# An RWKV-5 chunk kernel with a squared-ReLU FFN: two GpSimd DMA issues moved ahead of a weight cast, and two VectorE operations moved ahead of a third

## The chip, the cores and the metric

The kernel runs on one core of one Trainium2 chip. Its time is the device time of one execution in microseconds (us). The kernel before has three timed runs: 177.46, 177.65 and 178.44, median 177.65. The engines are called as in the profile: PE (TensorE matmul; PEld is its weight load), DVE (VectorE), ACT (ScalarE), POOL (GpSimd) and SP (SyncE, which here only issues DMAs).

## What is computed

The reference has two parts. The first is a linear attention with a decaying state, for 4 batches, 8 heads, 768 steps and head size 48:

```python
for t in range(S):
    kt, vt, rt = (k[:, :, t].copy(), v[:, :, t].copy(), r[:, :, t].copy())
    cur = np.einsum('bhd,bhe->bhde', u[None] * kt, vt)
    y[:, :, t] = np.einsum('bhd,bhde->bhe', rt, state + cur)
    state = w[None, :, :, None] * state + np.einsum('bhd,bhe->bhde', kt, vt)
```

Its result, as 3072 tokens of 384 values (heads side by side), goes through a feed-forward layer with `w_in` of 384 x 2048 and `w_out` of 2048 x 384:

```python
h = np.maximum(x @ w_in, 0.0)
return (h * h @ w_out).astype(np.float32)
```

## The kernel before

The sequence is cut into 24 units: unit `i` is chunk `i // 4` (128 steps) of batch `i % 4`, all heads. For each unit the kernel loads `r`, `k` and `v` (`ld`, line 320), scales them with powers of the decay (`kh`, L336, and `rh`, L339: products with the tables that `Wk` and `Wt` made on ACT), transposes them on PE (`T`, L363, copied by `Tc`), and forms the scores (`A`, L376), which are masked by `Bm` (L384). `Y` (L392 and L394) applies them and the state to `v`; `U` (L403) gives the state's update. The term with `u` is made beside that: `P0` (r times k, L342), `P1` (times `u`, L346), `du` (its sum over a head, L349), `dv` (times `v`, L354). `xs` (L411) adds both into the tokens, `X` and `xTc` transpose them.

The feed-forward part works on groups of one unit (groups 0 and 1) or two (the rest). `F1` (L445) multiplies tokens by `W1`, which is kept as 8 slices of 256 columns in bf16. `F1.g.s` fills one PSUM bank for group `g`: in groups 0 and 1 it takes the slices `2s` and `2s+1`, in the later groups the slice `s`. `re` (L453 on ACT or L455 on DVE) takes the ReLU, `sq` (L460 on ACT, L462 or L464 on DVE) squares it. `F2.i.q` (L472) multiplies by quarter `q` of `W2`, and `os` and `out` bring the unit's result out.

The weights arrive in two ways. `lW.0.s` (L324, SP) loads slice `s` of `W1` in float32 into one of four staging buffers, `wsa`, and `cW.0.s` casts it to bf16: on ACT (L260), except slice 7, which POOL casts (L262). `W.0.2` (slice 2 of `W1`) and `W.1.0` to `W.1.3` (the quarters of `W2`) are loaded and cast by DMAs that POOL issues (L333); they wait for nothing. In the profile q1 is the DMA queue on which SP issues, and q0 the one on which POOL issues.

The order of all work is written out by hand in `ORDER` (lines 20 to 107). Each word is one step, with its engine (P, D, A, G for POOL, S for SP) and the buffer slots that it takes; each engine does its steps in that order, and the framework adds the semaphore waits for data and buffers. `Z` are matmuls of the identity without a result, in the early gaps of PE. SP's early order is loads of units 0 to 3 mixed with `lW.0.6`, then `lW.0.1`, then `lW.0.0`, `.5`, `.7`, `.4`, then `wc` (two small DMAs for the last column table), `ld.k.4`, `lW.0.3`, `ld.r.4`, `ld.k.5`, `ld.r.5`. POOL's order in front of the first change is `P0.3`, `vb.2`, `P1.3`, `dv.2`, then `cW.0.7`, `W.1.0`, `W.0.2`, `W.1.1`, `WLm` (L314, which waits for ACT), `W.1.2`, `W.1.3`. On DVE the order at the second change is `shw` (the shuffle that spreads `w`, L283), `P0.1`, `kh.1`, `rh.1`, `shu` (the shuffle that spreads `u`, L286), `kh.0`. On PE the order after the first groups is `F1.1.0`, `F1.0.0`, `F1.1.3`, `F1.0.3`, `F1.0.2`, `F1.1.2`, four groups of `F1.2`, `F2.0.0` (the first that needs `W.1.0`), `F1.0.1` (the first that needs `W.0.2`, and the first with slice 3), `F1.2.3`, `F2.1.0`, `F1.1.1`, `F1.2.0`, `F2.0.1`, and so on.

`HELD` (lines 109 to 115) tells which buffers a step's slot numbers are for: of two steps that share a buffer, the one that stands first in `ORDER` names the slot.

Of the kernel before, what the change touches and what calls it, by code (L numbers as in the profile page):

```python
# [21 lines left out]
Wk:A/1 lW.0.6:S/0 kh.1:D/0 ld.v.1:S/0 rh.1:D shu:D ld.k.3:S/3 T.1:P/0 kh.0:D/1 Z.16.5:P P1.1:G Tc.1:A/0 kh.2:D/2  # L22
rh.0:D ld.v.3:S/1 WtS:A rh.2:D P0.2:G/1 A.1:P/1/2 WkS:A T.0:P/3 lW.0.1:S/1 Z.16.5:P P1.2:D ld.r.3:S/3 Tc.0:A/1
du.1:D/0 P0.0:D/2 cW.0.6:A ld.v.0:S/2 A.0:P/0/3 dv.1:G Bm.1.1:D/0 Z.6.5:P du.2:D/1 T.2:P/2 P1.0:G Bm.1.0:D/1
ld.v.2:S/3 Z.22.5:P Tc.2:A/2 Bm.0.0:D/2 Bm.0.1:D/3 lW.0.0:S/2 vb.1:A/0 lW.0.5:S/3 kh.3:D/3 Y.1:P/1 cW.0.1:A lW.0.7:S/0
A.2:P/0/2 xs.1:D/0 Z.4.5:P P0.3:G/3 vb.3:A/1 du.0:D/2 lW.0.4:S/1 X.1:P/3 Z.8.5:P rh.3:D wc:S xTc.1:A/0 Bm.2.0:D/4
vb.0:A/2 T.3:P/1 ld.k.4:S/4 dv.0:D Y.0:P/3 Z.13.5:P Tc.3:A/3 vb.2:G/3 Bm.2.1:D/5 P1.3:G xs.0:D/1 A.3:P/0/2 X.0:P/1
cW.0.0:A U.0:P/3 dv.2:G Bm.3.0:D/1 Z.6.7:P xTc.0:A/1 du.3:D/3 lW.0.3:S/2 F1.1.0:P/0 Bm.3.1:D/0 ld.r.4:S/4 F1.0.0:P/1
re.1.0:D/0 cW.0.7:G Y.2:P/0 Y.3:P/1 re.0.0:A/1 ld.k.5:S/5 xs.2:D/2 cW.0.5:A W.1.0:G dv.3:D F1.1.3:P/0 cW.0.4:A W.0.2:G
X.2:P/2 F1.0.3:P/1 re.1.3:D/2 ld.r.5:S/5 xTc.2:A/0 W.1.1:G U.2:P/0 xs.3:D/3 F1.0.2:P/0 re.0.3:A/3 sq.1.3:D2/0 WLcol:A  # L30
X.3:P/2 F1.1.2:P/1 re.0.2:D/4 xTc.3:A WLm:G U.3:P/1 F1.2.1:P/0 re.1.2:A/5 W.1.2:G sq.0.3:A0/1 F1.2.5:P/1 re.2.1:D/2
W.1.3:G sq.0.0:A0/2 U.1:P/2 S0.2:D re.2.5:A/3 F1.2.4:P/0 sq.0.2:D2/3 cW.0.3:A S0.0:D F1.2.7:P/1 re.2.4:D/1 sq.1.0:A0/4
F2.0.0:P/1 sq.2.5:D2/5 re.2.7:A/4 S0.3:D F1.0.1:P/0 F1.2.3:P/1 re.0.1:D/0 F2.1.0:P/0 S0.1:D re.2.3:A/3 F1.1.1:P/0
sq.1.2:D2/6 sq.0.1:D2/7 ld.k.7:S/6 F1.2.0:P/1 re.1.1:A/5 F2.0.1:P re.2.0:A/0 sq.1.1:D2/8 F1.2.2:P/0 sq.2.4:A0/9
sq.2.0:D1/10 F2.1.1:P kh.4:D/4 F1.2.6:P/1 ld.v.5:S/4 rh.4:D P0.4:D/4 F2.1.2:P ld.r.7:S/6 re.2.2:D/5 P1.4:G F2.0.2:P
re.2.6:D/1 sq.2.2:A0/11 F2.1.3:P ld.v.4:S/5 kh.5:G/5 sq.2.1:A0/12 sq.2.6:D1/13 F2.0.3:P os.1:A/0 du.4:D/4 ld.k.6:S/0
T.4:P/0 sq.2.3:A0/14 rh.5:D F2.2.0:P/0 os.0:A/1 P0.5:D/0 Tc.4:A/4 ld.r.6:S/0 T.5:P/3 P1.5:D F2.2.1:P kh.7:D/6 Tc.5:A/5
# [4 lines left out]
T.6:P/0 P0.7:D/2 os.2:A/2 A.7:P/1/2 S.5:D re.3.1:A/5 ld.r.8:S/1 F2.3.3:P du.6:D/2 P1.7:G Tc.6:A/0 Bm.7.1:D/0  # L42
F1.3.3:P/0 sq.3.0:A0/16 rh.9:G ld.r.10:S/3 os.3:D/3 F1.3.4:P/1 re.3.3:A/2 Bm.7.0:D/1 A.6:P/3/0 P0.9:G/3 du.7:D/1
re.3.4:A/1 XB.9:S/1 F1.3.5:P/0 Bm.6.1:D/3 sq.3.1:A0/17 dv.7:G F1.3.6:P/1 Bm.6.0:D/2 re.3.5:A/3 F2.5.0:P/0 dv.6:G
vb.6:A/7 ld.k.12:S/5 sq.3.3:A0/18 Y.7:P/2 out.3:S kh.10:D/3 re.3.6:A/4 Y.6:P/1 ld.v.8:S/3 S.4:G xs.7:D/1 F1.3.2:P/0
sq.3.5:A0/19 xs.6:D/2 F1.3.7:P/1 ld.v.11:S/1 kh.8:D/0 re.3.2:A/0 kh.15:D/4 U.6:P/0 X.6:P/3 sq.3.2:A0/20 X.7:P/2 rh.8:D
F2.4.0:P/1 ld.r.12:S/4 re.3.7:A/5 rh.10:D F2.5.1:P xTc.6:A/2 sq.3.4:D2/21 P1.9:D xTc.7:A U.7:P/1 T.8:P/3 vb.9:A/2
out.0:S P0.8:D/4 F1.4.0:P/0 ts.6:D/1 ld.k.11:S/0 Tc.8:A/2 P1.8:G ts.7:D/0 F1.4.4:P/1 ld.r.13:S/5 du.9:D/3 re.4.0:A/2
F2.5.2:P kh.12:G/5 re.4.4:A/3 F1.4.6:P/0 ld.r.11:S/0 sq.3.6:A0/23 sq.3.7:D2/22 vb.8:G/3 du.8:D/4 A.9:P/2/0
sq.4.4:A0/24 A.8:P/1/3 S.6:G re.4.6:A/0 F2.5.3:P ld.v.10:S/5 Bm.8.1:D/4 F1.4.3:P/1 dv.8:G Bm.8.0:D/5 os.5:A/3  # L50
ld.k.13:S/6 F1.4.5:P/0 Bm.9.1:D/1 re.4.3:A/1 dv.9:G Y.8:P/3 Bm.9.0:D/0 re.4.5:A/5 XB.10:S/3 F2.4.1:P P0.12:G/0
xs.8:D/3 sq.4.0:A0/25 Y.9:P/1 vb.11:A/1 kh.11:G/1 F1.4.1:P/1 xs.9:D/4 ld.v.13:S/4 X.8:P/0 F1.4.2:P/0 re.4.1:D/4
xTc.8:A/0 ld.r.15:S/6 F2.4.2:P rh.11:D sq.4.1:A0/26 P1.12:D X.9:P/2 vb.10:A/0 F1.4.7:P/1 P0.10:D/1 ld.k.20:S/2 xTc.9:A
sq.4.5:D2/27 F2.7.0:P/0 P0.11:D/2 re.4.7:A/3 ld.v.12:S/6 U.8:P/3 P1.10:D sq.4.3:A0/28 F2.4.3:P kh.13:D/6 re.4.2:A/2
F1.5.2:P/1 du.10:D/0 out.1:S os.4:A/1 rh.13:G sq.4.2:A0/29 ts.8:D/1 A.10:P/1/0 ld.k.17:S/1 F2.6.0:P/1 re.5.2:A/4
P1.11:G ld.k.14:S/5 F1.5.7:P/0 rh.12:G F1.5.1:P/1 du.11:D/1 ld.k.16:S/4 re.5.7:A/5 T.11:P/2 rh.15:D re.5.1:A/1
F1.5.0:P/0 dv.10:G Bm.10.1:D/3 Tc.11:A/4 ld.v.14:S/0 F1.5.5:P/1 vb.13:D/4 re.5.0:A/2 Bm.10.0:D/2 dv.11:G U.11:P/3
A.11:P/0/2 XB.13:S/5 sq.4.7:A0/2 F2.7.1:P S.7:D re.5.5:A/3 Bm.11.1:D/4 P0.15:G/3 Y.10:P/1 sq.5.2:A0/4 F2.6.1:P
XB.12:S/6 du.12:D/2 sq.5.5:A0/7 Bm.11.0:D/5 U.9:P/2 F1.5.6:P/0 kh.17:D/0 F2.6.2:P ld.r.14:S/2 ts.9:D/0 re.5.6:A/4
Y.11:P/0 sq.5.0:D2/8 sq.5.1:A0/6 out.2:S S.9:G xs.10:D/0 F1.5.3:P/1 sq.4.6:A0/3 ld.r.16:S/1 xs.11:D/2 F1.5.4:P/0  # L60
re.5.3:D/3 S.8:G X.10:P/2 U.10:P/1 XB.15:S/0 F2.7.2:P xTc.10:A/1 P1.15:D vb.14:A/5 F2.7.3:P ts.10:D/0 dv.12:G
ts.11:D/1 ld.r.17:S/3 X.11:P/0 F2.6.3:P os.7:A/0 kh.16:D/1 xTc.11:A kh.14:D/2 A.13:P/2/1 re.5.4:A/2 ld.k.18:S/0
A.12:P/3/0 F1.6.2:P/1 sq.5.3:A0/0 sq.5.4:D2/1 S.10:D os.6:A/2 F1.6.3:P/0 re.6.2:A/1 rh.14:D ld.v.18:S/3 F2.9.0:P/0
re.6.3:A/0 rh.16:D F1.6.6:P/1 sq.5.6:A0/10 sq.5.7:D2/12 XB.14:S/2 P0.13:D/4 F2.9.1:P Bm.13.0:D/1 P1.13:G F1.6.1:P/0
Bm.13.1:D/0 XB.16:S/1 F2.8.0:P/1 P0.14:G/1 Bm.12.1:D/3 re.6.1:A/2 F2.8.1:P Bm.12.0:D/2 sq.6.3:A0/11 P1.14:G
ld.r.18:S/0 sq.6.1:A0/14 A.15:P/2/1 F1.6.4:P/0 vb.12:A/7 out.6:S Bm.15.0:D/5 P0.17:G/2 re.6.6:A/3 ld.v.17:S/2 U.13:P/0
Y.12:P/3 du.13:D/4 re.6.4:A/5 F2.8.2:P rh.17:G xs.12:D/1 ld.v.15:S/5 F1.6.0:P/1 Bm.15.1:D/4 A.14:P/2/3 du.14:D/3
re.6.0:A/4 xX.12:S/2 U.12:P/1 dv.13:D F2.8.3:P sq.6.2:A0/9 kh.18:D/3 F1.6.5:P/0 Bm.14.0:D/3 XB.17:S/3 F1.6.7:P/1
S.11:D re.6.5:A/0 ts.13:D/0 F2.9.2:P os.8:A/2 out.7:S P0.18:D/0 sq.6.0:A0/5 Y.13:P/2 ts.12:D/1 ld.k.21:S/3
sq.6.6:A0/13 F2.9.3:P P1.18:G xs.13:D/3 sq.6.5:A0/15 ld.v.16:S/1 F2.10.0:P/1 Bm.14.1:D/2 dv.14:G X.13:P/0 du.15:D/0  # L70
F2.10.1:P ld.r.20:S/4 P0.16:G/4 re.6.7:D/2 xTc.13:A Y.14:P/1 vb.15:A/6 F1.7.5:P/0 kh.20:G/6 xs.14:D/4 ld.k.22:S/6
os.9:A/0 F1.7.6:P/1 S.12:D A.16:P/2/3 xX.14:S/0 re.7.6:A/1 P1.17:G A.17:P/0/1 F2.11.0:P/0 sq.6.7:A0/16 Bm.17.1:D/1
sq.6.4:A0/17 S.13:G F1.7.1:P/1 ld.v.20:S/6 Bm.16.1:D/0 re.7.5:A/4 F2.11.1:P ld.k.19:S/5 Bm.17.0:D/2 dv.15:G Y.15:P/1
re.7.1:D/3 ld.r.19:S/6 F1.7.0:P/0 xs.15:D/0 rh.20:G F1.7.3:P/1 re.7.0:A/0 ld.r.23:S/5 P1.16:D U.15:P/3 sq.7.1:A0/20
F2.10.2:P du.16:D/1 re.7.3:A/2 U.14:P/0 xX.15:S F1.7.2:P/0 P0.20:D/1 vb.16:A/3 dv.16:G Bm.16.0:D/3 sq.7.3:A0/18
F1.7.4:P/1 out.5:S re.7.2:A/5 rh.18:D F2.11.2:P vb.18:A/1 out.8:S sq.7.6:D2/21 re.7.4:A/3 F2.10.3:P sq.7.5:D2/19
ld.r.21:S/2 kh.19:D/5 vb.17:A/2 F1.7.7:P/0 ld.k.23:S/1 sq.7.4:A0/22 rh.19:D Y.16:P/1 kh.22:D/4 re.7.7:A/2 Y.17:P/2
XB.19:S/4 xs.16:D/2 sq.7.2:A0/23 F2.11.3:P kh.21:D/2 os.10:A/3 F1.8.2:P/1 du.17:D/2 sq.7.0:A0/26 XB.18:S/6 ts.14:D/1
F1.8.0:P/0 dv.17:G re.8.2:A/1 F2.12.0:P/1 os.11:A/2 re.8.0:D/4 vb.20:G/0 sq.8.2:A0/25 F1.8.3:P/1 xX.16:S/1 S.14:G
sq.7.7:A0/29 F2.13.0:P/0 re.8.3:A/3 P0.19:D/3 out.10:S U.17:P/1 F2.12.1:P ts.17:D/0 kh.23:G/0 ld.r.22:S/3 F1.8.7:P/0  # L80
xs.17:D/3 out.4:S du.18:D/4 F1.8.5:P/1 re.8.7:A/5 ts.15:D/1 F2.13.1:P re.8.5:A/0 S.15:D A.19:P/0/1 sq.8.7:A0/28
P1.19:D A.18:P/2/3 F1.8.1:P/0 Bm.19.1:D/5 xX.17:S rh.21:D F2.13.2:P re.8.1:A/1 P0.21:D/4 F1.8.4:P/1 ld.v.19:S/4
sq.8.3:A0/24 rh.23:D ld.v.22:S/0 F1.8.6:P/0 Bm.18.0:D/4 ld.v.21:S/5 U.18:P/1 rh.22:D F2.12.2:P re.8.6:A/2 Bm.18.1:D/0
sq.8.1:A0/27 F2.12.3:P XB.20:S/5 Bm.19.0:D/3 re.8.4:A/5 F1.9.1:P/0 S.17:D sq.8.6:A0/3 F2.13.3:P dv.18:D XB.21:S/2
# [25 lines left out]
    A=["bA{0}0", "bA{0}1"],  # L110
    ld=["{0}{1}"],
    lW=["ws{0}{1}"], kh=["rk{0}"], P0=["P{0}"], du=["dv{0}"], vb=["vb{0}"], T=["bT{0}"], Tc=["rkT{0}"], XB=["rkT{0}"],
    Bm=["Bm{0}{1}"], Y=["bY{0}"], xs=["xs{0}"], U=["bU{0}"], ts=["ts{0}"], X=["bX{0}"], re=["hr{0},{1}"], sq=["hq{0},{1}"],
    F1=["bH{0},{1}"], os=["os{0}"], Wk=["WkP"], Wt=["WtP"],
# [422 lines left out]
```

## Time and profile before

| | |
|---|---|
| median of three timed runs | 177.65 us (177.46 to 178.44) |
| span of the profiled execution | 175.6 us, about 2 us below the timed runs |
| granted clock of PE | 1.000 |
| busy: PE, DVE, ACT, POOL | 165.1, 140.6, 109.4, 69.2 us |
| DMA moved | 28.36 MB, mean 161 GB/s |
| first F1 matmul | 20.50 us |
| first F2 matmul | 30.08 us |

The span runs from the first to the last instruction that the profiler recorded; the timed run also holds what lies around it, so that differences are compared, not absolute times. In a line of the timeline stand the start and the length in us, the engine, the line of the kernel, the operation, its output and inputs, and in brackets how long the engine was idle before it and what ended that. A line of the waits tells who waited for whom: us in total, times, the longest. Matmuls overlap in the pipeline, so that the lengths of PE rows add up to a little more than the time between their starts. In the DMA view the share of a queue is the time of its packets over the time of 16 engines; reads and writes overlap, so that it can pass 100%.

### The profile page before, as it was taken

To read this page: it belongs to the slowest core of one execution; us is meant where nothing else is said; L and a number is where in the kernel's file an instruction comes from. 1 tells how busy PE (TensorE), PEld (TensorE's weight loads), DVE (VectorE), ACT (ScalarE), POOL (GpSimd) and SP (SyncE) were. 2 spreads that over 40 slices of the span, in tenths; PEclk is the share of its full clock that TensorE was granted. 3 is DMA by queue.
4 is the path that set the end of the run, shared out by engine and by line. 5 is a ranking of instruction groups with operands and counts; after the bars stand their busy time and mean duration, and the time that the engine had idled before them with its cause. 6 is when DMAs were issued, how large, how long until landed. Compare 5 with 4: busy or idle time off the path is not lost.

```text
span 175.6 us, 4601 instructions
## 1 busy us (share of the span) xinstructions
PE 165.1 (94%) x1813; PEld 127.0 (72%) x1813; DVE 140.6 (80%) x278; ACT 109.4 (62%) x203; POOL 69.2 (39%) x84
## 2 busy tenths in 40 slices
PE   4888797899999999999999999999999999999991
PEld 4767695666778778777767787777778677787760
DVE  4699877499899998999989899899988667853620
ACT  2479498249399987886668669669478132164401
POOL 4073582035358394926282960600960302000000
PEclk9999999999999999999999999999999999999999
DMA  5999999989899999999999979989971422110041
GB/s 105 218 217 236 315 231 187 192 166 220 163 210 106 246 207 134 232 159 242 170 162 214 212 142 223 155 203 191 199 157 26 157 90 62 33 45 0 4 169 55
DMA packets 102277, 28.36 MB, mean 161 GB/s; under 512 B 94824, under 2 KB 102256, under 8 KB 102256
## 3 DMA queue, kind: packets, MB, share of 16 engines
q1 hardware_dynamic: 100360, 26.10, 75.4%
q0 software_dynamic: 1744, 1.77, 6.1%
q8 instruction: 14, 0.23, 0.6%
q10 hardware_dynamic: 152, 0.20, 0.3%
q14 instruction: 7, 0.06, 0.1%
HBM read 20.46 MB, written 4.72 MB: 143 GB/s over the span
## 4 chain that ended last, share of the span: by engine, by line
PE 80%; DMA 10%; SPq 4%; POOL 1%; issue 1%; ACT 0%; POOLq 0%
PE bank L472 36%; PE bank L445 33%; DMA wsa<-in_moe_w_in_dram 6%; DMA W<-in_moe_w_in_dram 5%; SPq L320 4%; PE bank L376 3%; PE bank L394 2%; PE bank L392 2%; PE bank L403 2%; PE bank L363 2%; PE bank L429 1%; POOL W L262 0%; SPq L324 0%; POOL W L333 0%; ACT os L260 0%
## 5 line engine op out<-in xcount | busy, mean ns | idle before, releaser
L445 PE MATMUL bank<-xT,W 128*128 128x256 bf16 (+1 forms) x624 | 74.4, 264 | 1.6 <-ACT W L260 0.9
L472 PE MATMUL bank<-W,hq 128*128 128x384 bf16 x384 | 73.6, 326 | 1.0 <-DMA W<-in_moe_w_out_dram 1.0
L453 ACT ACTIVATE hr<-bank 128x512 bf16<-128x512 f32 x71 | 42.0, 597 | 38.9 <-PE bank L445 36.3
L445 PEld LDWEIGHTS <-W 128*128 128x128 bf16 x624 | 55.3, 98 | 12.3 <-ACT W L260 1.2
L472 PEld LDWEIGHTS <-hq 128*128 128x128 bf16 x384 | 35.6, 98 | 19.0 <-issue 1.2
L460 ACT ACTIVATE hq<-hr 128x512 bf16<-128x512 bf16 x57 | 34.7, 629 | 2.5 <-DVE hr L455 2.4
L384 DVE TENSOR_TENSOR Bm<-bank,maskJT 128x512 bf16<-128x512 f32 x48 | 31.4, 683 | 3.0 <-PE bank L376 3.0
L346 POOL TENSOR_TENSOR P<-P,ub 128x384 f32<-128x384 f32 x14 | 15.2, 1086 | 35.5 <-DVE P L342 29.8
L455 DVE TENSOR_SCALAR hr<-bank 128x512 bf16<-128x512 f32 x25 | 17.1, 689 | 11.9 <-PE bank L445 8.3
L354 POOL TENSOR_TENSOR dv<-ldv,du 128x384 f32<-128x384 f32 x19 | 16.6, 886 | 23.7 <-DVE du L349 21.6
L464 DVE TENSOR_TENSOR hq<-hr 128x512 bf16<-128x512 bf16 x35 | 15.0, 457 | 1.7 <-ACT hr L453 1.7
L411 DVE TENSOR_TENSOR xs<-bank,dv 128x384 bf16<-128x384 f32 x24 | 13.2, 553 | 2.8 <-PE bank L394 2.2
L260 ACT COPY os<-bank 128x384 f32<-128x384 f32 x18 | 8.6, 477 | 8.1 <-PE bank L472 8.1
L481 PE MATMUL bank<-identity 128*128 128x128 bf16 x139 | 11.0, 242 | 2.3 <-POOL identity masks.py:199 2.3
L349 DVE TENSOR_REDUCE du<-P 128x8 f32<-128x384 f32 x24 | 12.9, 544 | 0.2 <-POOL P L346 0.2
L342 POOL TENSOR_TENSOR P<-ldr,ldk 128x384 f32<-128x384 f32 x11 | 11.3, 1024 | 2.4 <-DMA ldr<-in_r_dram 2.4
L260 ACT COPY rkT<-bank 128x1024 bf16<-128x1024 bf16 x10 | 10.1, 1015 | 2.8 <-PE bank L363 2.7
L481 PEld LDWEIGHTS <-identity 128*128 128x128 bf16 x139 | 9.7, 111 | 2.5 <-POOL identity masks.py:199 2.3
L424 POOL TENSOR_TENSOR S0W<-ts,WLm 128x384 bf16<-128x384 f32 x7 | 7.4, 1060 | 10.0 <-PE bank L472 6.7
L394 PE MATMUL bank<-vb,Bm 128*128 128x48 bf16 x192 | 10.8, 183 | 0.4 <-ACT vb L260 0.3
L394 PEld LDWEIGHTS <-Bm 128*128 128x128 bf16 x192 | 9.5, 96 | 1.4 <-issue 0.6
L260 ACT CAST vb<-ldv 128x384 bf16<-128x384 f32 x19 | 9.6, 512 | 0.0
(61 smaller groups left out, 163.8 us busy)
## 6 DMA issues: line engine op xcount, KB each, us to landing
ldr<-in_r_dram SPq DMA_DIRECT2D x24, 192.0 KB, 4.0
ldk<-in_k_dram SPq DMA_DIRECT2D x24, 192.0 KB, 4.1
ldv<-in_v_dram SPq DMA_DIRECT2D x24, 192.0 KB, 3.8
out_dram<-os SPq DMA_DIRECT2D x23, 192.0 KB, 2.1
wsa<-in_moe_w_in_dram SPq DMA_DIRECT2D x7, 384.0 KB, 4.8
W<-in_moe_w_out_dram POOLq DMA_DIRECT2D x4, 384.0 KB, 10.2
rkT<-rk SPq DMA_TRANSPOSE x14, 4.2
W<-in_moe_w_in_dram POOLq DMA_DIRECT2D x1, 192.0 KB, 8.1
```

The costliest lines, as they stand in the source:

```text
L260: e.copy(o, a)
L346: e.tensor_mul(t, t, ub)
L354: e.tensor_mul(dvb[slot[f"dv{i}"]], loaded("v", i), t)
L384: e.tensor_mul(Bmb[slot[f"Bm{i}{h}"]], heads(bank(f"bA{i}{h}"), 128), mask_b)
L394: e.matmul(y[:, hc, D * h : D * (h + 1)], m[h][:, hc, :], vb[:, 2 * hc + h, :], start=(c == 0), stop=True, skip_group_check=True,)
L445: e.matmul(hp[:, fi, :], W1[f // 2][:, c, 128 * (f % 2) : 128 * (f % 2 + 1)], xt[:, c, :], start=(c == 0), stop=(c == CCH - 1), skip_group ...
L453: e.activation(hr, hp, AF.Relu)
L455: e.tensor_scalar_max(hr, hp, 0.0)
L460: e.activation(hq, hr, AF.Square)
L464: e.tensor_mul(hq, hr, hr)
L472: e.matmul(bank(f"bO{i}", "bO")[:, 0:d_model], hqb[slot[f"hq{g},{f // m}"]][:, at : at + L], W2[q][:, f % 4, :], start=(f == 0), stop=(f = ...
L481: e.matmul(banks[b][:, 0:128], identity, identity, start=True, stop=True, skip_group_check=True)
```

## The change

Three groups of words move in `ORDER`, and `rh` is entered in `HELD`, since `rh.1` is now the step that names the slot of `rk1`. No step is added or taken away. The rest of `ORDER` is only wrapped anew; it has one line less, so that lines of the changed kernel behind it are numbered one lower (L332 for L333, and so on). In the words of `ORDER`:

```diff
 ld.r.2:S/2 Wt:A/0 P0.1:D/0
+shu:D
 Wk:A/1 lW.0.6:S/0
-kh.1:D/0 ld.v.1:S/0 rh.1:D shu:D
+rh.1:D/0 kh.1:D ld.v.1:S/0
 ld.k.3:S/3 T.1:P/0 kh.0:D/1
...
 ld.r.4:S/4 F1.0.0:P/1 re.1.0:D/0
+W.1.0:G W.0.2:G
 cW.0.7:G Y.2:P/0 Y.3:P/1 re.0.0:A/1 ld.k.5:S/5 xs.2:D/2 cW.0.5:A
-W.1.0:G
 dv.3:D F1.1.3:P/0 cW.0.4:A
-W.0.2:G
 X.2:P/2 F1.0.3:P/1 re.1.3:D/2
...
-    lW=["ws{0}{1}"], kh=["rk{0}"], P0=["P{0}"], du=["dv{0}"], vb=["vb{0}"], T=["bT{0}"], Tc=["rkT{0}"], XB=["rkT{0}"],
+    lW=["ws{0}{1}"], kh=["rk{0}"], rh=["rk{0}"], P0=["P{0}"], du=["dv{0}"], vb=["vb{0}"], T=["bT{0}"], Tc=["rkT{0}"], XB=["rkT{0}"],
```

On POOL the order becomes `dv.2`, `W.1.0`, `W.0.2`, `cW.0.7`, `W.1.1`; on DVE it becomes `P0.1`, `shu`, `rh.1`, `kh.1`, `kh.0`. The orders of PE, ACT and SP stay as they are.

## The prediction

> **What bounds the kernel now.** I read first the busy times of the page, then the waits of TensorE, then the chain and the timelines around the two places that the change touches.
>
> ```profile
> PE 165.1 (94%) x1813; PEld 127.0 (72%) x1813; DVE 140.6 (80%) x278; ACT 109.4 (62%) x203; POOL 69.2 (39%) x84
> ```
>
> TensorE (PE) is busy 94% of 175.6 us at full granted clock (the PEclk row is all nines), so about 10 us are idle. The waits of TensorE from 20 us to the end are these, in all:
>
> ```profile
> PE bank L472 <- DMA W<-in_moe_w_out_dram: 1.0, 1, 1.0
> PE bank L445 <- ACT W L260: 0.9, 1, 0.9
> PE bank L445 <- DMA W<-in_moe_w_in_dram: 0.7, 1, 0.7
> ```
>
> So nothing holds TensorE after its last one, and what the change does to the end of the kernel is what it does to these three. The timeline of PE and GpSimd places them (start, length, and in brackets the idle time ahead):
>
> ```profile
> 20.50 1.51 PE L445 MATMUL bank<-xT,W 128*128 128x128 bf16 x24 [0.88 <-ACT W L260]
> ...
> 30.08 0.81 PE L472 MATMUL bank<-W,hq 128*128 128x384 bf16 x4 [1.03 <-DMA W<-in_moe_w_out_dram]
> 31.63 0.56 PE L445 MATMUL bank<-xT,W 128*128 128x128 bf16 x7 [0.74 <-DMA W<-in_moe_w_in_dram]
> ```
>
> ```profile
> 19.49 0.83 POOL L354 TENSOR_TENSOR dv<-ldv,du 128x384 f32<-128x384 f32 x1
> 21.82 0.88 POOL L262 CAST W<-wsa 128x768 bf16<-128x768 f32 x1 [1.49 <-DMA wsa<-in_moe_w_in_dram]
> 22.64 0.89 POOL L333 DMA_DIRECT2D W<-in_moe_w_out_dram  x1
> 23.53 0.76 POOL L333 DMA_DIRECT2D W<-in_moe_w_in_dram  x1
> 24.29 0.78 POOL L333 DMA_DIRECT2D W<-in_moe_w_out_dram  x1
> ```
>
> TensorE waits at 29.05 for the first quarter of W2 (F2.0.0; it lands at 22.64 + 7.4 = 30.04) and, one group later, for slice 2 of W1 (F1.0.1; 23.53 + 8.06 = 31.59). GpSimd sat idle for 1.49 us ahead of the cast of slice 7, and the two issues stood behind that cast. That wait for the cast is what the change takes out of their way.
>
> **The move of the two issues.** They wait for nothing, so they run when `dv.2` ends: 19.49 + 0.83 = 20.32. The first takes 0.89 (to 21.21), the second 0.76 (to 21.97). Both start 2.32 us earlier. The cast, whose data were there at about 21.8, starts at 21.97 instead of 21.82, so 0.15 late, and `W.1.1` behind it at 22.85 instead of 24.29. The late cast holds F1.1.3 (22.74) by 0.15. That is covered: two groups on, TensorE's weight load waits 0.16 us for ScalarE's cast of slice 4 (until 24.27), which does not move. Without that cover it would cost 0.15. `W.1.2` and `W.1.3` (26.18, 26.87) wait for WLm and stay where they are.
>
> An earlier issue is not yet an earlier landing. The DMA view by stretches (packets, MB, share of 16 engines):
>
> ```profile
> q1 hardware_dynamic: 1916, 0.61, 111.4%
> ```
> ```profile
> q0 software_dynamic: 250, 0.32, 94.9%
> q1 hardware_dynamic: 110, 0.02, 10.7%
> ```
> ```profile
> q0 software_dynamic: 381, 0.29, 91.5%
> q1 hardware_dynamic: 378, 0.07, 33.1%
> ```
>
> These are 22.9 to 25.2, 26 to 28 and 30 to 32 us. GpSimd's queue (q0) sends its first packet at about 25.2 (none before; 3 from 25.2 to 25.4), 2.6 us after the issue started. So it would now start at 22.9, into engines that SP's queue (q1) keeps full until 25.2. What q1 has left there is the rest of slice 3 of W1 (`lW.0.3`, issued 20.47, landed 25.03) and `ld.r.4` (landed 25.80). Of 1916 packets with 0.61 MB, if they have 1024 and 192 bytes (rows of 256 and 48 floats), about 290 are slice 3's: 18 for each engine.
>
> How much that delays q0 no row shows; the ends are 0 (q0 is served as if alone) and 2.3 us (q1 drains first, and q0 starts at 25.2 as before). From 30 to 32 the queues took turns, 381 packets against 378, so I reckon by turns: slice 3's 18 packets per engine at 50 ns (18 to 20 us, where it is almost all such rows: 99.7% of 32 engine-us over 643 packets) are 0.9 us, and I take 1.0, since `ld.r.4`'s short packets (28 ns from 30 to 32) shared with q0 then too. Slice 2 then lands at 31.59 - 2.3 + 1.0 = 30.3, the W2 quarter at 28.7 or a little before.
>
> The arbitration is also stated by the Trainium skill ("DMA: Bandwidth & Descriptors", section on queues, rings and completion order): each engine goes round the queues packet by packet. By it alone the delay is that of the turns, as above; the stretch from 26 to 28, 250 packets against 110, does not show it.
>
> The sum at the wait: F2.0.0 finds its weights (28.7 before 29.05), which gives 1.03. F1.0.1 could start 0.81 later, at 29.86, and waits for 30.3: of 0.74 it keeps 0.44. Together 1.03 + 0.74 - 0.44 = 1.33 us. What is late next, in the chain's times: W2's second quarter (landed 34.26, used at 35.11), third (36.53, used 37.72), fourth (38.75, used at 37.72 + 1.30 = 39.02). All of these must come 1.33 earlier less 0.85, 1.2 and 0.27. q0 is never empty between (its packets lag its issues by far more than 2.6 us), so they move with the queue's 1.3 us, and the fourth just fits (37.45 against 37.69).
>
> **The move on VectorE.** `shu` (0.58) and `rh.1` (0.55) go ahead of `kh.1`, no instruction is added. VectorE stood idle for 1.27 us there:
>
> ```profile
> 4.96 0.54 DVE L342 TENSOR_TENSOR P<-ldr,ldk 128x384 f32<-128x384 f32 x1
> 6.78 0.55 DVE L336 TENSOR_TENSOR rk<-ldk,bank 128x384 bf16<-128x384 f32 x1 [1.27 <-ACT bank L292]
> ```
>
> `shu` fits into that gap if `u` has landed (its issue lies between those of loads that landed at 4.4 and 6.1), and `rh.1` needs only the table that ScalarE ends at 6.24. `kh.1` then starts at 6.8 as now, or 0.5 later at worst; its followers come up to 0.9 earlier, until loads stop them (`ld.r.2` lands at 9.11). I cost it at nothing either way: F1 starts at 20.50 on the cast of slice 0, whose load lands at 19.54 after an issue at 14.72 that the loads ahead on SP's queue set. If that cover were gone, it would be worth -0.9 to +0.5.
>
> **Rivals.**
> *A, the engines are full, so nothing is gained.* If q1's backlog is served first, or the cost of sharing is 2.3 us and not 1.0, W2_0 and W1_2 land where they do now: 177.65, perhaps 0.15 more for the cast. For it: 111.4% busy from 22.9 to 25.2, and q0's first packet came just as q1 ran low. Against: by turns a packet of q0 (94.9% of 32 engine-us over 250, 121 ns) gets more of the engine than the 50 ns one it takes turns with. The Trainium skill has the same warning (same page, "Rules for kernel authors"): spreading transfers over issuing engines gives no bandwidth, since all share the 16 engines.
> *B, the gain is given back later.* After 32 us TensorE has no gap, but VectorE, ScalarE and the loads follow closely (vb.4 starts at 42.80 with `ld.v.4` landed at 41.94). If they cannot follow 1.3 us earlier, the time is again near 177.6. Against: VectorE and ScalarE themselves waited for TensorE there (2.39 and 3.26 us until about 33).
> *C, slower: q1 is starved.* Slice 3 and `ld.r.4` now meet q0's long packets; from 26 to 28 q1 got only 110 packets against 250, and a load issued at 23.24 landed 14.3 us later. Slice 3 is cast at 28.07 on ScalarE for the second half of F1.0.1 (31.96 now). It has 3 us to spare, and it costs nothing until it lands after 31.96 - 0.82 = 31.1. If it lands only with the third software transfer, at about 33, TensorE stands 1.9 us longer than now: 179.6.
> *D, the moves do nothing* because the issue was not what was late: contradicted by 2.32 us of plain idleness and issue, but its result is that of A.
>
> **How the numbers follow.** The span of 175.6 would be 174.3; the timed runs lie about 2 us above it, and 1.33 off their median of 177.65 gives 176.3; I say 176.4, since the fourth W2 quarter only just fits. Chances: forecast 0.57 (175.7 to 176.75, from the cost of sharing between 0 and 1.3), A and D 0.15, B 0.11, C 0.17. Best end: 1.03 + 0.74 = 1.77 off, 175.9, and noise of the median 0.2. To leave out no more than 2 in 10 the range takes in A and B and the mild part of C, up to 178.2. A measurement of this kernel tells about 0.5%, 0.9 us, from no change: faster 0.57, same 0.25, slower 0.18.
>
> **What would show it.** Right: POOL's two DMA issues at 20.3 and 21.2, the cast at about 22.0; no wait of PE at L472 for W2, one of about 0.4 us at L445; q0's first packet near 22.9; slice 3 landed between 26 and 28.5. Wrong: q0's first packet still at 25 (A), a wait of ScalarE for wsa after 28 us or of VectorE for ldr at about 36 (C), new gaps of PE behind 35 us (B), F1 starting at another time than 20.5 (the VectorE move counts).

## The result and the profile after

| | before | after |
|---|---|---|
| median of 20 runs each, same chip | 177.25 us (176.13 to 178.44) | 175.94 us (174.52 to 179.37) |
| span of the profiled execution | 175.6 us | 173.6 us |
| its own time | about 2 us above the span | 175.28 us |

The ratio of after to before is 0.9936, with a 95% interval from 0.9915 to 0.9957: 1.1 us less, between 0.8 and 1.5. (The ratio is taken without the executions that came more than 1.5% above the fastest of their kernel, 4 of the 20 of after and up to 5 of 12 below, which is why it can differ from the quotient of the medians.) The two profiled executions differ by more, 2.0 us; where that comes from is told below.

The busy times on the page of the kernel after:

```profile
PE 165.2 (95%) x1813; PEld 127.7 (74%) x1813; DVE 140.5 (81%) x278; ACT 109.5 (63%) x203; POOL 69.1 (40%) x84
```

The work is the same, and TensorE's idle time is 8.4 us where it was 10.5. All its waits from 20 us to the end are now these (us in total, times, the longest):

```profile
PE bank L444 <- ACT W L259: 1.0, 1, 1.0
PE bank L444 <- ACT hr L452: 0.2, 1, 0.2
```

Both waits for a DMA into `W` are gone. The first line was there before (F1's start); the second is new. GpSimd's timeline shows the cause (start, length, engine and line):

```profile
19.16 0.82 POOL L353 TENSOR_TENSOR dv<-ldv,du 128x384 f32<-128x384 f32 x1
19.93 0.89 POOL L332 DMA_DIRECT2D W<-in_moe_w_out_dram  x1
20.82 0.76 POOL L332 DMA_DIRECT2D W<-in_moe_w_in_dram  x1
21.58 0.90 POOL L261 CAST W<-wsa 128x768 bf16<-128x768 f32 x1
22.40 0.78 POOL L332 DMA_DIRECT2D W<-in_moe_w_out_dram  x1
```

The issues stand 2.71 us earlier than before (19.93 for 22.64, 20.82 for 23.53): the first 0.33 of that is that `dv.2` itself began at 19.16 and not at 19.49. The cast started 0.11 after slice 7 of `W1` had landed (21.47). TensorE's timeline over the same stretch:

```profile
20.21 1.51 PE L444 MATMUL bank<-xT,W 128*128 128x128 bf16 x24 [0.96 <-ACT W L259]
...
28.60 0.81 PE L471 MATMUL bank<-W,hq 128*128 128x384 bf16 x4
29.25 0.83 PE L444 MATMUL bank<-xT,W 128*128 128x128 bf16 x12
30.29 0.82 PE L444 MATMUL bank<-xT,W 128*128 128x256 bf16 x6 [0.20 <-ACT hr L452]
30.94 0.81 PE L471 MATMUL bank<-W,hq 128*128 128x384 bf16 x4
```

The last of these rows is F2.1.0, which before stood here:

```profile
32.97 0.81 PE L472 MATMUL bank<-W,hq 128*128 128x384 bf16 x4
```

F2.0.0 starts at 28.60 and F1.0.1 at 29.25, neither with a wait; their weights landed at 27.17 and 29.11 (30.04 and 31.59 before). F2.1.0 starts at 30.94, 2.03 us earlier than before (32.97), and the last F2 at 169.60, 2.04 us earlier than before (171.64): nothing is given back behind that point.

The 2.03 us can be added up from starts. With no wait, F2.0.0 stands 28.60 - 20.21 = 8.39 behind the start of F1. Before, it stood 30.08 - 20.50 = 9.58 behind: a wait of 1.19. F1.0.1 stood 1.55 behind F2.0.0, now 0.65: a wait of 0.90. These two, 2.09, are gone. F1 itself started 0.29 earlier. Against that, F1.2.3 came late: from F1.0.1 to F2.1.0 it is now 1.69 where it was 1.34, so 0.35 lost. 2.09 + 0.29 - 0.35 = 2.03. (The brackets in the timeline say less, 1.03 + 0.74 for the old waits and 0.20 for the new one, because the last matmuls before a wait still run in the pipeline while the next ones are kept back.)

Where the 0.35 come from is in ScalarE's timeline of after:

```profile
28.39 0.83 ACT L259 CAST W<-wsa 128x768 bf16<-128x768 f32 x1 [0.51 <-DMA wsa<-in_moe_w_in_dram]
29.13 0.62 ACT L459 ACTIVATE hq<-hr 128x512 bf16<-128x512 bf16 x1
29.66 0.57 ACT L452 ACTIVATE hr<-bank 128x512 bf16<-128x512 f32 x1
```

Slice 3 of `W1` landed at 28.37 (25.03 before), 8.19 us after its issue where it had taken 4.56: its packets now share the DMA engines with those of GpSimd's queue. The profiles below bear this out: slice 3, issued at the same place, took 7.0 to 8.2 us in the seven profiles with an issue directly ahead of the cast, and 4.3 to 5.6 in the three profiles of the old order. The cast waits 0.51 for it, and behind the cast in ScalarE's order stands `re.2.7` (the L452 line), which has to empty a PSUM bank before F1.2.3 can start.

The DMA view (packets, MB, share of 16 engines) from 19.93 to 21.66, from the issue to the first packet of GpSimd's queue, then from 21.6 to 24, and from 26.5 to 29, after the change:

```profile
q1 hardware_dynamic: 1008, 0.59, 111.6%
q0 software_dynamic: 1, 0.00, 0.5%
```
```profile
q1 hardware_dynamic: 1156, 0.27, 59.2%
q0 software_dynamic: 125, 0.19, 53.6%
```
```profile
q0 software_dynamic: 524, 0.33, 89.4%
q1 hardware_dynamic: 553, 0.13, 39.3%
```

q0 got in while q1 kept every engine full, so it had not waited for q1 to run dry. Just behind its first packet the two do not alternate packet for packet (125 to 1156), though each takes about half of the engines' time. From 26.5 to 29 they nearly do (524 to 553), and the queue with the long packets moves 2.5 times the bytes.

### The profile page after: what moved, and what is told of

It is laid out like the page before. It is cut to its first block, busy times and chain, and to the rows that moved or that the text cites. A ratio compares the mean times of both kernels' runs of the same rounds, so it can differ in the third digit from the quotient of the medians.

```text
span 173.6 us, 4600 instructions
## 1 busy us (share of the span) xinstructions
PE 165.2 (95%) x1813; PEld 127.7 (74%) x1813; DVE 140.5 (81%) x278; ACT 109.5 (63%) x203; POOL 69.1 (40%) x84
## 3 DMA queue, kind: packets, MB, share of 16 engines
q0 software_dynamic: 1744, 1.77, 6.1%
## 4 chain that ended last, share of the span: by engine, by line
PE 83%; SPq 6%; POOL 3%; DMA 3%; DVE 1%; issue 1%; ACT 1%; POOLq 0%
PE bank L471 36%; PE bank L444 34%; SPq L319 5%; PE bank L375 3%; DMA ldv<-in_v_dram 3%; PE bank L393 2%; PE bank L391 2%; PE bank L402 2%; PE bank L362 2%; PE bank L428 1%; POOL W L332 1%; SPq L323 1%; DVE hr L454 1%; POOL P L345 1%; POOL W L261 1%
## 5 line engine op out<-in xcount | busy, mean ns | idle before, releaser
L452 ACT ACTIVATE hr<-bank 128x512 bf16<-128x512 f32 x71 | 42.0, 597 | 36.6 <-PE bank L444 33.9
L480 PE MATMUL bank<-identity 128*128 128x128 bf16 x139 | 11.7, 252 | 2.3 <-POOL identity masks.py:199 2.3
L480 PEld LDWEIGHTS <-identity 128*128 128x128 bf16 x139 | 10.3, 115 | 2.5 <-POOL identity masks.py:199 2.3
```

Of the source, the lines that this page charges most:

```text
L452: e.activation(hr, hp, AF.Relu)
L480: e.matmul(banks[b][:, 0:128], identity, identity, start=True, stop=True, skip_group_check=True)
```

## The experiments

Theory 1: the whole gain is that of the two issues; from its first packet q0 takes turns with q1, so that what an earlier issue wins is set by the queues' turns and by what it holds back on q1; the move on VectorE does nothing. The rivals are told with the runs that bear on them. Each ratio is to the kernel before, timed beside it on the same chip. Diffs are in the words of `ORDER`.

**The issues alone.** The kernel before, with only the two issues moved:

```diff
 F1.0.0:P/1 re.1.0:D/0
+W.1.0:G W.0.2:G
 cW.0.7:G
 ...
 cW.0.5:A
-W.1.0:G
 dv.3:D F1.1.3:P/0 cW.0.4:A
-W.0.2:G
```

> Theory 1: the two issues ahead of the cast make the whole gain, by taking both waits of PE for q0 (1.03 and 0.74 us before) away; F1 then starts where the loads let it, 20.2 to 20.5 us, and the time is 0.993 to 0.995 of the kernel before, as with the whole change (0.9936). Rival 2: the VectorE move made F1 start at 20.21 instead of 20.50; then F1 starts at 20.5 here and the ratio is about 0.995 to 0.996. In both the new wait of about 0.2 us at F1.2.3 is there.

Measured: 0.9926 (0.9881 to 0.9971). TensorE's timeline of this kernel up to 31 us, and the cast of slice 3 on ScalarE:

```profile
20.25 1.51 PE L444 MATMUL bank<-xT,W 128*128 128x128 bf16 x24 [0.84 <-ACT W L259]
...
28.65 0.81 PE L471 MATMUL bank<-W,hq 128*128 128x384 bf16 x4
29.30 1.49 PE L444 MATMUL bank<-xT,W 128*128 128x128 bf16 x18
```
```profile
27.88 0.83 ACT L259 CAST W<-wsa 128x768 bf16<-128x768 f32 x1
```

Without the move on VectorE, F1 starts at 20.25 and both waits for `W` are gone: the gain is the issues'. (This execution, with a span of 177.9 us, lost 4.7 us behind F2.1.0, 2.6 of them in a wait of TensorE for ScalarE's copy of an output, `os`, until 100.75; only what stands ahead of that is read here.) Slice 3 happened to land at 27.86 here, 0.5 earlier than in after; the cast has no wait, F1.0.1 and F1.2.3 run through as one row, and F2.1.0 starts 1.32 behind F1.0.1 (30.62 - 29.30), as before the change; the wait of 0.2 that was expected here did not come. So the 0.35 of after hang on when slice 3 lands, within half a microsecond.

**VectorE alone.** The kernel after with the two issues put back, timed twice:

```diff
-W.1.0:G W.0.2:G
 cW.0.7:G
 ...
 cW.0.5:A
+W.1.0:G
 dv.3:D F1.1.3:P/0 cW.0.4:A
+W.0.2:G
```

> Theory 1: the VectorE move is hidden behind the load of slice 0 of W1: kh.0 about 0.9 us earlier, F1 still at 20.2 to 20.5 us, both waits of PE for q0 as before (1.0 and 0.7 us), ratio 0.999 to 1.001. Rival 2: F1 starts 0.3 us earlier and so does everything behind it, ratio 0.998.

> The same kernel as with the VectorE move alone, since 0.9969 (0.9927 to 1.001) did not tell 1.000 from 0.998. Theory 1: 1.000, in any case within 0.999 to 1.001; PE's waits for q0 as before. Rival 2: 0.998 or less. By the two runs together.

Measured: 0.9969 (0.9927 to 1.001), then 0.9999 (0.9971 to 1.0027). No effect can be told from none; the two together, weighted by their intervals, give 0.999 (0.9966 to 1.0013), so that the 0.998 of the rival isn't excluded by the times. TensorE's timeline of the first of the two, where F1 started at 20.21 as in after:

```profile
31.36 0.81 PE L471 MATMUL bank<-W,hq 128*128 128x384 bf16 x4 [1.43 <-DMA W<-in_moe_w_out_dram]
32.75 1.50 PE L444 MATMUL bank<-xT,W 128*128 128x128 bf16 x18 [0.59 <-DMA W<-in_moe_w_in_dram]
```

The waits that the issues had taken away are back. The second execution shows neither of them. Its timeline of TensorE:

```profile
21.20 2.74 PE L444 MATMUL bank<-xT,W 128*128 128x128 bf16 x24 [1.61 <-ACT W L259]
...
30.81 0.81 PE L471 MATMUL bank<-W,hq 128*128 128x384 bf16 x4
```

Here slice 0 of `W1` landed late (20.26; 19.54 in the profile of before), so F1 started at 21.20, and the clock then fell (told below). By the time F2.0.0 was its turn, its weights, issued at 23.35 as in the old order, had been there since 29.37, and slice 2 since 31.13 when F1.0.1 started at 31.46. At full clock, 8.39 and 9.04 us behind F1, the two would have been due at 29.59 and 30.24, and F1.0.1 would have waited (an estimate): it took the late start and the slow clock together to hide the waits.

That explains why two profiles can differ by 2.0 us and the medians by 1.1: the two waits are not the same in every execution. They hang on F1's start, which scatters from 19.7 to 21.6 over these profiles (leaving out the kernel with the issues behind `P1.0`, in which it comes for another reason), on the clock, and on the landing: in the first of the two executions slice 7 landed at 22.49 and not at 21.76, so the issues behind its cast came only at 23.72. Counted from F1's start, the W2 quarter and slice 2 landed at 9.54 and 11.09, 11.11 and 12.50, 8.17 and 9.93 in the three profiles of the old order, and at 5.3 to 7.0 and 7.4 to 8.9 in the five with both issues ahead of the cast and the loads as they were; at full clock they are due at 8.39 and 9.04. That an execution of the old order can be without the waits is shown once, not counted over all.

**One issue ahead of the cast.** The kernel after, with `W.0.2` directly behind the cast:

```diff
-W.1.0:G W.0.2:G cW.0.7:G
+W.1.0:G cW.0.7:G W.0.2:G
```

> Only the W2 quarter stays ahead of the cast; slice 2 of W1 is issued behind it, at about 22.4 us. Theory 1, served by queue: the packets of the W2 quarter keep q0 busy until about 25, so an issue at 22.4 is not late for its turn; slice 2 lands at about 29, PE waits for neither, ratio as with the whole change, 0.993 to 0.995. Rival 3, landing follows the issue by about 8.2 us (8.06 before, 8.29 after): slice 2 lands at 30.6, PE waits about 1.3 us for it, ratio 0.996 to 0.997.

Measured: 0.9926 (0.9884 to 0.9968). On GpSimd and on TensorE:

```profile
23.45 0.76 POOL L332 DMA_DIRECT2D W<-in_moe_w_in_dram  x1
```
```profile
30.57 1.50 PE L444 MATMUL bank<-xT,W 128*128 128x128 bf16 x18 [0.26 <-DMA W<-in_moe_w_in_dram]
```

Slice 2 landed at 30.52, 7.07 after its issue, where in after it took 8.29 (20.82 to 29.11). Counted from F1's start, the issue came 1.78 us later than in after and the landing 0.56 later. So the landing does not follow the issue by a fixed time, as a rival had it; it follows the first quarter through the queue. It landed later than the 29 that Theory 1 had, and TensorE waits 0.26 for it. The gain can't be told from that of both issues, so it is there with the first alone ahead of the cast.

**Still earlier.** The kernel after with both issues behind `P0.3`, and, in another kernel, behind `P1.0`:

```diff
 P0.3:G/3
+W.1.0:G W.0.2:G
 ...
-W.1.0:G W.0.2:G
 cW.0.7:G
```

```diff
 P1.0:G
+W.1.0:G W.0.2:G
 ...
-W.1.0:G W.0.2:G
 cW.0.7:G
```

> Both issues run at about 16.6 us, behind P0.3, where GpSimd waits anyway; q0's packets begin at about 18.3 and meet slices 5, 7 and 4 of W1 on q1. Turns, packet by packet: the slices are held up by 2 to 3.6 us, the casts of 7, 5 and 4 wait, PE waits 2 to 3 us at F1.1.3 or F1.0.2, and ratio is 1.000 to 1.008 of before though the waits at 29 and 30 us are gone. If instead q1 is hardly slowed, PE waits for nothing behind 21 us and the ratio is 0.991 to 0.993. If q0 is held until q1 runs low, it is as after: 0.9936.

> Both issues run at about 13.1 us, behind P1.0, where q1 carries short packets of loads and the slices 0, 5, 7 and 4 are still to be issued. Theory 1 (turns, and what is fetched early holds back what is needed first): slice 0 is late, F1 starts 1.5 to 3 us later than 20.3, and the ratio is 1.00 to 1.01. For q0's first packet: 1.7 to 2.7 us after the issue as in four of the five runs so far if the 4.15 us of the run with the issues behind P0.3 come from q1's long packets ahead of it; about 4 us again if it is the time that an early issue takes for another reason.

Measured: 1.0012 (0.9973 to 1.005) and 1.0136 (1.0098 to 1.0173), the second above its forecast. The gain is lost, then more than lost. TensorE's timeline of the first, and ScalarE's cast of slice 4:

```profile
21.50 2.68 PE L444 MATMUL bank<-xT,W 128*128 128x128 bf16 x24 [1.62 <-ACT W L259]
...
27.37 0.84 PE L444 MATMUL bank<-xT,W 128*128 128x128 bf16 x12 [0.72 <-ACT W L259]
```
```profile
26.44 0.88 ACT L259 CAST W<-wsa 128x768 bf16<-128x768 f32 x1 [0.84 <-DMA wsa<-in_moe_w_in_dram]
```

Here q0's first packet came at 21.08, behind the landing of slice 0 (20.54). So the late F1 (21.50), and the clock of 0.70 that followed it, are not shown to come from the issues; F1 was as late without such issues (21.56 with the larger fill, below). Behind that packet slice 7 landed at 23.79 (21.47 in after), and slice 4 late enough to cost TensorE 0.72 us, less than the 2 to 3 that was expected of the turns. How much of the lost gain is q0's doing stays open for this place.

ScalarE's timeline and the DMA view from 14.8 to 18 us of the second, and below them the same stretch of before:

```profile
22.78 0.89 ACT L259 CAST W<-wsa 128x768 bf16<-128x768 f32 x1 [2.47 <-DMA wsa<-in_moe_w_in_dram]
```
```profile
q0 software_dynamic: 309, 0.40, 82.0%
q1 hardware_dynamic: 891, 0.17, 28.8%
```
```profile
q1 hardware_dynamic: 2491, 0.75, 105.1%
```

With q0 at work from 14.80 us, q1 moves 0.17 MB where it moved 0.75. Slice 0, which F1 starts on, lands at 22.75 and not at 19.54, and F1 starts at 23.72. The mechanism of rival C (q1 held back by q0's long packets) is real; it bites the loads that are due while q0 works. With the issues at 19.93, as in the profile of after, slice 0 is through (19.25), and slice 3 and `ld.r.4` are left to pay.

**A third issue ahead of the cast.** The kernel after with `W.1.1` there too; this takes away the time that covers the late cast:

```diff
-W.1.0:G W.0.2:G cW.0.7:G
+W.1.0:G W.0.2:G W.1.1:G cW.0.7:G
 ...
-W.1.1:G
```

> The second W2 quarter goes ahead of the cast as well, so that the cast of slice 7 runs some 0.8 us later than with the change, at about 22.4. Theory 1: only some 0.16 us of such a delay is covered (the wait for the cast of slice 4), F1.1.3 waits about 0.7 us and the second quarter, which was in time, brings nothing: 0.5 to 0.7 us slower than with the change, ratio 0.9965 to 0.998 of before. Rival 5: the cast has more cover than that, and the ratio is as with the change, 0.993 to 0.994.

Measured: 0.9989 (0.9956 to 1.0021). The cast started at 23.21, 0.88 after its data (22.33). In the profiled execution TensorE does not wait for it, but F1 had started late there (21.00) and ran at a reduced clock (0.62 from 20 to 24 us), so that it needed slice 7 later. The ratio lies above both that the change has given (0.9936, and 0.9976 below), but the intervals overlap: what a later cast costs is not settled. (Of the executions with a mean granted clock of 0.992 or more, the medians are 176.70 us here, for 8, and 177.03 for the kernel before, for 21: the clock alone does not explain the small gain.)

**Slice 3 out of the way.** The kernel after with a fifth staging buffer (`wsa=5`), and slice 3 loaded directly behind slice 4, timed twice:

```diff
 lW.0.4:S/1
+lW.0.3:S/4
 ...
-lW.0.3:S/2
```

> Slice 3 of W1 gets a fifth staging buffer and is issued right behind slice 4, at about 17 us instead of 20.2, so that it is through before q0's packets start. Theory 1: the new wait in the changed kernel (ScalarE 0.51 us for slice 3, then PE at F1.2.3, 0.39 us by its start) comes from slice 3 taking turns with q0; here slice 3 lands before 25 us, no cast waits behind 22.5 us, and the time is 0.990 to 0.993 of the kernel before. Rival 4: the wait is made up later or replaced (the two small loads and ld.k.4 now come after slice 3), and the ratio stays at 0.9936 or is above it.

> The kernel with slice 3 of W1 early, in a fifth buffer, once more, since its first profile shows another execution (948.6 us). Theory 1: slice 3 lands before 25 us, ScalarE's cast of it and PE at F1.2.3 wait for nothing; the time is at best 0.002 below the change. Rival 4, which the first ratio (0.9939) favours: the wait is gone but its 0.2 to 0.4 us are not seen in the time, because in most executions slice 3 was in time anyway (one of three profiles with an early issue shows ScalarE waiting).

Measured: 0.9939 (0.9911 to 0.9966), then 0.9915 (0.9879 to 0.995). The profiled execution of the first took 950 us, for which its records give no reason, and isn't read. In the second, slice 3 landed at 25.11. ScalarE's timeline and TensorE's:

```profile
25.52 0.20 ACT L307 ACTIVATE wcol<-wcol 128x4 f32<-128x4 f32 x1 [1.00 <-DMA wcol<-in_w_dram]
...
28.45 0.82 ACT L259 CAST W<-wsa 128x768 bf16<-128x768 f32 x1
```
```profile
22.54 0.51 PE L444 MATMUL bank<-xT,W 128*128 128x128 bf16 x6 [0.55 <-POOL W L261]
...
26.38 1.47 PE L444 MATMUL bank<-xT,W 128*128 128x256 bf16 x12 [0.65 <-ACT xT L259]
```

The cast of slice 3 no longer waits; instead ScalarE waits 1.00 for the two small loads of `wcol`, which now come behind one more slice on SP's queue, and the copy of `xT` behind it holds TensorE 0.65. One late load is traded for another. The second is the lowest ratio of the study, but neither can be told from that of the change itself.

**The clock in the gap ahead of F1.** The kernel after without the fill `Z.13.5` and `Z.6.7` just ahead of F1, with more of it, and unchanged:

```diff
-Z.13.5:P
 ...
-Z.6.7:P
```

```diff
-Z.6.7:P
+Z.20.7:P
```

> The changed kernel without the 19 matmuls of the identity that fill PE's gaps at 17.1 and 18.8 us. Theory on the spread of the times: in the profiles where PE idled 1.6 us or more ahead of F1, the granted clock fell to 0.62 to 0.70 from 20 to 24 us, and F2.0.0 came 9.6 us behind F1's start and not 8.4. So here the idle stretch gets longer, the clock falls in most executions, and the time is 1.0 to 1.3 us over the change (ratio to before about 1.000). Rival: the clock falls for reasons outside the kernel; then the time and the clock are as with the change, 0.9936.

> The changed kernel with 20 matmuls of the identity instead of 6 ahead of F1, about 0.75 us more, so that PE idles about 0.2 us there and not 0.96. Theory: no execution has the early fall of the clock, and the executions that had it come down by 1.2 us; the others stay, or lose up to 0.5 us when slice 0 is early. Ratio 0.991 to 0.994. Rival: the clock falls as often as before, ratio 0.9936 or above.

> The changed kernel beside the other three, for their comparison. All theories: 0.9915 to 0.9957 of the kernel before; no wait of PE for the first W2 quarter or for slice 2 of W1.

Measured: 0.9997 (0.9962 to 1.0033) without, 0.9954 (0.9924 to 0.9983) with more, 0.9976 (0.9943 to 1.0009) for the change itself. TensorE without the fill (its lines are one lower), and the table of stretches from 20 us on (length, PE busy, granted clock, DMA share, GB/s):

```profile
20.99 2.74 PE L443 MATMUL bank<-xT,W 128*128 128x128 bf16 x24 [2.11 <-ACT W L258]
...
31.43 0.81 PE L470 MATMUL bank<-W,hq 128*128 128x384 bf16 x4
```
```profile
20.00:24.00 4.00, 3.01 (x35) 0.50 1.14 258
24.00:28.00 4.00, 4.00 (x62) 0.72 1.24 246
```

After 2.11 us of idle TensorE the granted clock is 0.50, the first 24 matmuls of F1 take 2.74 us and not 1.51, and F2.0.0 comes 10.44 behind F1's start and not 8.39: 2.05 us lost. TensorE in the change's own second profile, and its stretch:

```profile
21.11 1.51 PE L444 MATMUL bank<-xT,W 128*128 128x128 bf16 x24 [1.67 <-ACT W L259]
```
```profile
20.00:24.00 4.00, 2.83 (x57) 1.00 1.15 250
```

Here 1.67 us of idle time left the clock alone (the last section comes back to it). The mean granted clock of an execution was below 0.992 in 8 of 12 executions without the fill, in 2 of 12 with the change's fill and in none of 12 with more. Within the kernel without fill, the 8 have a median of 177.24 us and the other 4 of 175.73. The mean does not say where the clock fell: in the profile of the issues alone, with a mean of 0.987, it fell at 101.61 us, behind the wait for `os`. The fill is worth having; that more of it beats the change is not shown, since the intervals overlap, and the 0.991 to 0.994 expected of it were missed (in its profile slice 0 landed at 20.61, and TensorE idled 1.12 us in spite of the fill).

Is the gain of the change the clock's? The kernel before has the same fill, and 4 of its 31 executions here were below 0.992. Of those at 0.992 or more, the medians are 176.63 us for before (27 executions) and 176.12 for the change (10); beside the issues alone they were 177.12 (25) and 175.71 (7). So a gain of 0.5 to 1.4 us is there at full clock too.

## Why the prediction was right

The forecast was 176.4 us, 1.25 below the median it started from; measured are 175.94, and a gain of 1.1 (0.8 to 1.5). Most of the way from 176.4 to 175.94 is the kernel before, whose 20 runs have a median 0.4 below that of the first three. The cause of the gain, shown by the issues alone and VectorE alone, is the one named. The second measurement, 0.9976, reaches to no change; with both issues at these places the issues alone, the early slice 3 and the larger fill gave 0.9915 to 0.9954, and only the kernels with a third issue ahead of the cast (0.9989) and with the fill taken out (0.9997) gave more. By its steps:

- *Issues 2.3 us earlier, cast 0.15 late*: right (2.71, of which 0.33 by an earlier `dv.2`; the cast 0.11). That the delay is covered showed in after; the price without cover is open.
- *q0's first packet 2.6 us after the issue, at 22.9*: the term that failed. It came at 21.66: 0.39 by the earlier issue, and 0.84 because the packet followed after 1.73 us.
- *Sharing costs q0 1.0 us*: right in this pair of profiles, not settled beyond it. From first packet to landing, the W2 quarter took 5.51 for 4.83 (0.68 more) and slice 2 7.45 for 6.38 (1.07 more). But slice 2 took 5.3 to 6.6 us in the three profiles of the old order and 6.1 to 7.5 in the five with both issues ahead of the cast, so the two overlap; and the packets just behind q0's first were not the turns that the working took (125 to 1156). Rival A falls: q0 was served with q1 at 111.6%, and the W2 quarter landed 2.87 us earlier.
- *F1.0.1 keeps a wait of 0.44*: it kept none, since slice 2 landed at 29.11 and not at 30.3, which is the queue's earlier start again. And the two waits held 2.09 us by starts, not the 1.77 of their idle rows. That left the sum as it was: by starts the two are due at 28.89 and 29.54, and 1.19 + 0.90 less a kept wait of 0.76 is the same 1.33, which is how much earlier slice 2 was to land.
- *Slice 3 lands from 26 to 28.5 and costs nothing until 31.1*: the landing is right (28.37), the cost is not. The step looked at the matmuls that need slice 3, and not at `re.2.7`, which stands behind the cast on ScalarE and which TensorE needs sooner: 0.35 lost.
- *What is late next*: right. The fourth W2 quarter landed at 36.35 and was used at 36.82. `ld.r.4` landed at 34.31 (25.80 before) for a use at 34.82; 0.5 us were left.
- *VectorE at nothing*: no effect was found. The shuffle went into the gap (DVE timeline of after):

```profile
5.36 0.57 DVE L285 STREAM_SHUFFLE ub<-urow 128x384 f32<-128x384 f32 x1
6.20 0.56 DVE L338 TENSOR_TENSOR rk<-ldr,bank 128x384 bf16<-128x384 f32 x1 [0.27 <-ACT bank L297]
6.71 1.48 DVE L335 TENSOR_TENSOR rk<-ldk,bank 128x384 bf16<-128x384 f32 x3
```

  `kh.1` starts at 6.71 (6.78 before), and F1 starts with slice 0's cast, with the move or without it. The prediction had named an F1 at another time than 20.5 as a sign that the move counts; F1 stood at 20.21 in after, but at 20.25 without the move.
- *Rival B, given back later*: not seen; the last F2 is as much earlier as F2.1.0.

What no step of it had: F1's start is not the same from one execution to the next. The prediction took one profile's waits for those of all. In the pair of profiles the change is worth 2.09 - 0.35 = 1.74 us, more than the 1.33 of the sum; over all executions it is 1.1, less than that. That the forecast lies so near is luck in part: a landing put 1.2 us too late, and waits taken to be the same in every execution, err in opposite directions.

## What to carry to other kernels

A DMA issue that waits for nothing should not stand behind an instruction that waits, on the engine that issues it; but the earliest place is not the best one, since from its first packet it shares the DMA engines with loads that may be due sooner: of the places tried here, the best was about where the load that starts the main work had got through. When a load is to come later, ask not only who reads it, but who stands behind its reader in that engine's queue. And read a gain from more than one profile where a wait depends on when something else happens to start.

## What was not expected of the hardware

**The clock falls after short gaps.** Gaps ahead of F1 of 0.29 to 1.12 us left the granted clock at 1.00; after 1.61, 1.62, 1.79 and 2.11 us it fell (to 0.65, 0.70, 0.62 and 0.50 in the stretch from 20 to 24 us), after 1.67 us it did not. (With the issues behind `P1.0` it was 0.50 there too, after gaps of 1.30 and 1.74 us from 16 us on and one of 0.47 ahead of F1.) No single length decides. The Trainium skill ("TensorE: Matmul & The Clock Gate", "Why this matters for your kernels") asks for no gaps above about 3 us; the traces do not agree with that as a safe bound. Part 1 of the same page of the Trainium skill says that activity is judged over windows that run freely.

The traces show steps of that kind: each fall in the clock's records starts a whole number of steps of 3.41 us behind the first record of the full clock and, ahead of the kernel's end, lasts one step or two; the steps lie otherwise in each execution. Cut along them (length, PE busy, granted clock, DMA share, GB/s), first VectorE alone the second time, then the change's own second profile:

```profile
17.82:21.24 3.42, 1.72 (x30) 1.00 0.97 312
21.24:24.65 3.41, 3.41 (x43) 0.50 0.97 244
```
```profile
18.61:22.03 3.42, 1.75 (x30) 1.00 1.07 293
22.03:25.44 3.41, 3.35 (x68) 1.00 1.12 187
```

Over all profiles PE was busy for 0.85 to 1.84 us of the step ahead of a fall inside the kernel, and for at least 1.59 in every step without a fall behind it. So the work in a step, somewhere near half of it, tells more than a gap's length, and the same gap can count or not by where it lies. Where the line lies can't be said: the two ranges overlap, and the ends of the matmuls are modelled.

**How long q0 takes to start.** From the first issue's start to q0's first packet it took 1.60 to 2.70 us in eleven profiles (1.60, 1.73 and 1.96 the three shortest), 3.76 in the one with slice 3 early and 4.15 in the one with the issues behind `P0.3`, the issue itself about 0.9 of that. The Trainium skill ("DMA: Bandwidth & Descriptors", "Latency and other measured facts") gives about 1 us to the first byte for this path; counted from the end of the issue, only the three shortest of these (0.7 to 1.1) agree with it. What sets it is open; full engines alone do not, since 1.73 was measured with q1 at 111.6% and 4.15 with it at 91.7%.
